# Folding the first two batches on TensorE, and new slots for the transforms of the others

## The chip, the cores and the metric

The kernel runs on one core of one Trainium2 chip. The metric is the device time of one execution in microseconds (us); lower is better. Before the change it was 667.26 us (median of three runs, 667.0 to 668.79). PE is TensorE, DVE is VectorE, ACT is ScalarE, POOL is GpSimd, SP is SyncE; PSUM is what TensorE writes to. The kernel's inputs and output stay in DRAM.

## The reference

Two stages, one after the other: the real part of a 2D Fourier transform of each of 8 batches, and a gated two-layer network on every token.

```python
def _attn_ref(x):                      # x: 8 x 3008 x 256, float32
    X = np.fft.fft(x, axis=1)
    X = np.fft.fft(X, axis=2)
    return X.real.astype(np.float32)

def _moe_ref(x, w_gate, w_val, w_out): # 24064 tokens, 256 -> 1536 -> 256
    g = x @ w_gate
    gelu = 0.5 * g * (1.0 + erf(g / sqrt(2)))
    val = x @ w_val
    return (gelu * val @ w_out).astype(np.float32)
```

## The kernel before

The transform is made of matmuls. Its input is first *folded*: each row of x is added to its mirror in time and in channel, which halves the work that follows. So x is loaded twice, forward by a plain DMA from SP's queue and mirrored by a gather from POOL's queue. Each load of 8 of the 17 parts is 768 KB. Batch 0 is folded on DVE, all others on POOL.

```python
    raw = [const_pool.tile([NPX, NJ, C], FP32, name=f"x_raw{i}") for i in range(2)]  # forward, mirror
    def load_part(b, k):
        j0, nj = ((9, 8), (1, 8), (0, 1))[k]
        load_forward(b, j0, nj)        # SP queue, 768 KB
        load_mirror(b, j0, nj)         # POOL queue, gather
    def fold_ops(b, j0, nj, eng):
        # ... first, second: sums over time and channel of raw[FORWARD], raw[MIRROR]
        if half_folded(b):             # b < 2: the last combination is left to the channel stage
            return [first, second]
        return [first, second, combine(0, ALU.add), combine(1, ALU.subtract)]
```

Then come stage 1 (over time), the channel stage, and the last stage (`tp_e`, `tp_o`), whose results ACT copies from PSUM into `EO_sb`, the input of the network. Three groups of columns are made per batch. For one row of `O` the copy is not enough: `tp_y` computes it, writes it to DRAM (`yrow`), and `tp_rows` reads it back, spread over all partitions into `EB_sb` and into one row of `EO_sb`.

```python
    def s1(b, jg, g, engine="A"):                       # stage 1, batches 0 and 1
        # ...
            for q, js in enumerate(JG[jg]):
                for j in js:
                    nc.tensor.matmul(ps[:, q * 96 : (q + 1) * 96], eo[:, j, g, :], G[:, j, :], ...)
    def tp_y(b, gi):
        # ... a 4 x 128 matmul, copied to yr, then
            nc.sync.dma_start(out=<4 x 128 of yrow in DRAM>, in_=yr[:, :])
    def tp_rows(b, gi):
        # ...
            nc.sync.dma_start(out=<EB_sb, group gi, 128 partitions>, in_=<yrow>)
            nc.sync.dma_start(out=<EO_sb, O half, group gi, 1 partition>, in_=<yrow>)
```

The network is 288 blocks in a row, 36 for each batch. A block makes one gelu pair. I call a block a *slot* and count them from 0. The rest of the work is hung into slots by a plan. The transform of batch b runs in the 36 slots of the network of batch b-1, so batch 2's in slots 36 to 71.

```python
    def plan():                                         # fill[s], pool[s]: work of slot s
        # ...
        for b in range(1, B):
            s0 = (b - 1) * NS                           # NS = 36
            # ops: 20 folds (10 for b = 1)
            first, n = {1: (11, 5), 2: (24, 28)}.get(b, (s0 - 16, 32))
            slot_of = [first + i * n // len(ops) for i in range(len(ops))]
            # ...
            if b + 1 < B:
                for k, piece in ((0, 1), (1, 3), (2, 4)):
                    at(fill, slot_of[piece * per + 1] + 1, lambda b=b, k=k: load_part(b + 1, k))
            # ... stage 1 after the folds; then the 9 items tp_y, tp_e, tp_o of 3 groups,
            #     the last of them in slot s0 + 33, about one a slot; tp_rows one slot after each group
```

## Time and profile before

Each line of the page gives busy times or shares of the span. First the page of the kernel before: busy time of PE and of ACT, PE's busy share in 40 equal slices (a digit is tenths), the clock that PE was granted in the same slices, and the chain of work that ended last.

```profile
span 666.5 us, 12960 instructions
PE 622.6 (93%) x4253; PEld 411.0 (62%) x4253; DVE 585.4 (88%) x946; ACT 432.0 (65%) x843; POOL 505.9 (76%) x509
PE   2888999999979999899979999799999999999997
...
PEclk9998999999989999899998999899999999999999
...
PE 76%; POOL 6%; DMA 6%; ACT 4%; issue 3%; DVE 2%; SPq 1%; POOLq 0%; ACTq 0%; DVEq 0%
```

PE is the engine that is full, but after its opening it falls to 7, 8, 7 and 7 in four slices some 80 us apart (a slice is 16.7 us; they begin at 183, 267, 333 and 417 us), and in each of them or the next one the clock falls to 8. In a single-core kernel that is PE-bound almost everywhere, the thing to read is where PE is *not* busy. The Trainium skill says in "Perfetto Trace Analysis", Identifying the Most-Contended Engine, that busy time of matmuls is a poor measure of distance to the roofline; that agrees here, since in the last of the windows at the end of this section PE is busy 2.00 of 2.00 us at half of its clock.

The chain of waits in order of time (start, length, what) names the gaps. These are its DMA pieces:

```profile
178.97 8.65 DMA EO_sb<-yrow
258.96 8.31 DMA EO_sb<-yrow
338.58 8.29 DMA EO_sb<-yrow
419.77 7.99 DMA EO_sb<-yrow
```

Around the first of them, the timeline shows who waited. Columns are start, busy time, engine, line and operation, what is written and read, and in brackets the engine's idle time before it with what ended it. SPq and POOLq lines are DMA issues; the data lands later.

```profile
177.30 0.95 POOL L145 DMA_INDIRECT x_raw<-in_x_dram,idx  x1
...
177.86 0.53 SPq L139 DMA_DIRECT2D x_raw<-in_x_dram  x1
178.49 0.40 SPq L555 DMA_DIRECT2D EB_sb<-yrow  x1
178.97 0.23 SPq L557 DMA_DIRECT2D EO_sb<-yrow  x1
179.42 0.25 SPq L547 DMA_DIRECT2D yrow<-yrow_sb  x1
...
187.71 0.57 ACT L521 ACTIVATE EO_sb<-ps_dft 128x481 bf16<-128x481 f32 x1 [4.60 <-DMA EO_sb<-yrow]
188.18 0.57 ACT L605 ACTIVATE gelu_sb<-ps_g 128x481 bf16<-128x481 f32 x1
...
189.26 0.77 PE L589 MATMUL ps_g<-EO_sb,W_sb 128*128 128x481 bf16 x3 [3.96 <-ACT gelu_sb L614]
```

The gather and the forward load of batch 4 start at 177.3 and 177.9; right behind them, after the row's read into `EB_sb`, goes the read of the one row of `EO_sb` (issued 178.97; I call it the row read), which lands at 187.6. ACT's copy of the next group into the same tile waits for it 4.6 us, both gelus stand behind the copy in ACT's order, and PE idles 4 us. What that does to the clock is in the busy time by windows. A line has the window, then busy time (and instructions) of PE, weight loads, DVE, ACT and POOL, then the granted clock, the DMA share and GB/s.

```profile
186.00:188.00 2.00, 0.00 (x0) 0.00 (x0) 0.19 (x1) 0.29 (x1) 0.55 (x1) 1.00 0.90 200
190.00:192.00 2.00, 2.00 (x12) 1.25 (x10) 1.20 (x2) 1.02 (x3) 0.39 (x1) 0.64 0.20 30
192.00:194.00 2.00, 2.00 (x7) 0.89 (x6) 1.11 (x3) 1.60 (x3) 1.12 (x2) 0.50 0.13 33
```

After 4 us without work, PE is granted half of its clock for some 3.4 us. That is the clock gate that the Trainium skill describes in "TensorE: Matmul & The Clock Gate", Part 1.

### The profile page before, as it was taken

What the parts mean: (1) busy time and instruction counts of PE and PEld (TensorE: products, weight loads), DVE (VectorE), ACT (ScalarE), POOL (GpSimd) and SP (SyncE); (2) the same over time, 40 slices, a digit from 0 to 9 for tenths busy, and PEclk for the clock granted to TensorE, in tenths of its full rate; (3) what the DMA queues carried; (4) which work ended last, traced back from release to release, by engine and by line L of the source; (5) the groups of instructions that cost most, each with busy time, mean ns of one, the idle gap of its engine ahead of it and who ended that gap; (6) DMA issues with size and microseconds to landing.
All of it is one profiled execution on the core that took longest, in us unless ns stands there. A gap on an engine that the chain in (4) does not pass through costs nothing.

```text
span 666.5 us, 12960 instructions
## 1 busy us (share of the span) xinstructions
PE 622.6 (93%) x4253; PEld 411.0 (62%) x4253; DVE 585.4 (88%) x946; ACT 432.0 (65%) x843; POOL 505.9 (76%) x509
## 2 busy tenths in 40 slices
PE   2888999999979999899979999799999999999997
PEld 1544666666646666566656666466666666666666
DVE  7697799999969998699968999699999999999992
ACT  3685676766746665666656667476677766766661
POOL 8449789988969699686987879688799865556551
PEclk9998999999989999899998999899999999999999
DMA  9942715453435336253361642626322133211112
GB/s 216 223 106 60 186 45 130 108 141 106 100 83 129 96 102 144 54 130 101 98 148 33 146 124 64 142 51 170 104 61 53 40 92 95 60 45 43 49 48 77
DMA packets 52332, 66.74 MB, mean 100 GB/s; under 512 B 7865, under 2 KB 47180, under 8 KB 49580
## 3 DMA queue, kind: packets, MB, share of 16 engines
q1 hardware_dynamic: 46024, 49.69, 28.7%
q0 software_dynamic: 5648, 15.73, 10.6%
q8 instruction: 33, 0.54, 0.4%
q10 hardware_dynamic: 592, 0.49, 0.3%
q14 instruction: 35, 0.29, 0.1%
HBM read 38.86 MB, written 29.38 MB: 102 GB/s over the span
## 4 chain that ended last, share of the span: by engine, by line
PE 76%; POOL 6%; DMA 6%; ACT 4%; issue 3%; DVE 2%; SPq 1%; POOLq 0%; ACTq 0%; DVEq 0%
PE ps_o L662 31%; PE ps_g L589 24%; PE ps_v L589 15%; DMA EO_sb<-yrow 5%; POOL h_sb L638 2%; PE ps_dft L475 2%; POOL eo_sb L194 2%; ACT gelu_sb L614 1%; ACT gelu_sb L605 1%; PE ps_dft L511 1%; SPq L583 1%; POOL x_raw L145 1%; PE ps_dft L456 1%; DMA out_dram<-out_sb 1%; DVE v_sb L636 1%
## 5 line engine op out<-in xcount | busy, mean ns | idle before, releaser
L638 POOL TENSOR_TENSOR h_sb<-gelu_sb,v_sb 128x512 bf16<-128x512 bf16 (+1 forms) x288 | 329.2, 1145 | 141.6 <-DVE v_sb L636 115.4
L662 PE MATMUL ps_o<-Wo_sb,h_sb 128*128 128x256 bf16 (+1 forms) x2232 | 338.8, 275 | 0.0
L662 PEld LDWEIGHTS <-h_sb 128*128 128x128 bf16 (+1 forms) x2304 | 231.0, 101 | 114.3 <-issue 4.0
L623 DVE SCALAR_TENSOR_TENSOR ve_sb<-EB_sb,yw,ps_v 128x512 f32<-128x512 bf16 (+1 forms) x288 | 212.3, 737 | 56.7 <-PE ps_v L589 55.5
L589 PE MATMUL ps_g<-EO_sb,W_sb 128*128 128x512 bf16 (+1 forms) x864 | 234.0, 380 | 16.4 <-ACT gelu_sb L614 16.3
L605 ACT ACTIVATE gelu_sb<-ps_g 128x512 bf16<-128x512 f32 (+1 forms) x288 | 169.7, 589 | 88.5 <-PE ps_g L589 85.5
L589 PE MATMUL ps_v<-EO_sb,W_sb 128*128 128x512 bf16 (+1 forms) x576 | 216.9, 380 | 0.5 <-ACT W_sb L390 0.5
L634 DVE TENSOR_TENSOR h_sb<-gelu_sb,ps_v 128x512 bf16<-128x512 bf16 (+1 forms) x288 | 195.3, 678 | 4.4 <-PE ps_v L589 3.4
L589 PEld LDWEIGHTS <-W_sb 128*128 128x128 bf16 x1440 | 137.4, 98 | 97.6 <-issue 20.2
L636 DVE SCALAR_TENSOR_TENSOR v_sb<-ve_sb,ps_v 128x512 f32<-128x512 f32 (+1 forms) x288 | 192.8, 670 | 0.0
L614 ACT ACTIVATE gelu_sb<-ps_g 128x512 bf16<-128x512 f32 (+1 forms) x288 | 169.2, 588 | 0.0
L681 ACT ACTIVATE out_sb<-ps_o 128x512 f32<-128x512 f32 x92 | 54.9, 597 | 40.6 <-PE ps_o L662 40.5
L194 POOL TENSOR_TENSOR eo_sb<-ab_sb 94x512 bf16<-94x512 f32 (+1 forms) x60 | 66.6, 1110 | 0.1
L521 ACT ACTIVATE EO_sb<-ps_dft 128x512 bf16<-128x512 f32 (+1 forms) x44 | 25.9, 589 | 31.0 <-DMA EO_sb<-yrow 17.4
L478 ACT ACTIVATE S_sb<-ps_dft 96x512 bf16<-96x512 f32 x48 | 28.4, 591 | 26.2 <-PE ps_dft L475 26.2
L187 POOL TENSOR_TENSOR ab_sb<-x_raw,x_raw 94x508 f32<-94x508 f32 (+1 forms) x30 | 32.9, 1097 | 0.0
L190 POOL TENSOR_TENSOR ab_sb<-x_raw,x_raw 94x508 f32<-94x508 f32 (+1 forms) x30 | 32.9, 1096 | 0.0
L145 POOL DMA_INDIRECT x_raw<-in_x_dram,idx x27 | 26.1, 966 | 5.4 <-issue 1.5
L475 PE MATMUL ps_dft<-eo_sb,G 94*96 94x256 bf16 x102 | 19.0, 272 | 2.0 <-POOL eo_sb L194 2.0
L511 PE MATMUL ps_dft<-TP,Z_sb 128*128 128x128 bf16 (+1 forms) x188 | 18.2, 220 | 1.0 <-DVE Z_sb L463 1.0
L511 PEld LDWEIGHTS <-Z_sb 128*128 128x128 bf16 x192 | 15.0, 100 | 3.0 <-DVE Z_sb L463 1.2
L475 PEld LDWEIGHTS <-G 94*96 94x96 bf16 x102 | 12.0, 124 | 3.2 <-issue 2.8
(117 smaller groups left out, 157.9 us busy)
## 6 DMA issues: line engine op xcount, KB each, us to landing
out_dram<-out_sb SPq DMA_DIRECT2D x361, 64.0 KB
x_raw<-in_x_dram SPq DMA_DIRECT2D x12, 768.0 KB
Z_sb<-z SPq DMA_DIRECT2D x6, 768.0 KB
z<-S_sb SPq DMA_DIRECT2D x6, 576.0 KB
EB_sb<-yrow SPq DMA_DIRECT2D x14, 128.0 KB
x_raw<-in_x_dram SPq DMA_DIRECT2D x2, 640.0 KB
x_raw<-in_x_dram SPq DMA_DIRECT2D x3, 384.0 KB
z<-S_sb SPq DMA_DIRECT2D x6, 192.0 KB
```

The lines of the kernel that those rows point to most:

```text
L194: eng.tensor_tensor(_sub(eo, [[C, nj], [1, 128]], j0 * C + g * 128), ab(0, 0, [[1, 128]]), ab(1, 0, [[1, 128]]), op=op)
L475: nc.tensor.matmul(ps[:96, q * C : (q + 1) * C], G[:, j, :], _sub(eo, [[1, C]], j * C), start=(j == js[0]), stop=(j == js[-1]))
L511: nc.tensor.matmul(ps[:, o : o + n], st["Z"][:, pair, g * 128 : g * 128 + 128], _sub(TP, [[1, n]], g * 128), start=True, stop=True)
L589: nc.tensor.matmul(ps[:, :n], W[nm, part][:, fs], src, start=start, stop=stop, **kw)
L605: nc.scalar.activation(gl[:, 0, :n], pg[:, :n], AF.Gelu)
L614: nc.scalar.activation(_sub(gl, [[-1, n]], TOK + n - 1), pg[:, :n], AF.Gelu)
L623: nc.vector.scalar_tensor_tensor(ve[:, :n], EB_bufs[b][:, c0 : c0 + n], yw[:, fc : fc + 1], pv[:, :n], op0=ALU.mult, op1=ALU.add)
L634: nc.vector.tensor_tensor(st["h"][:, fc, 0, :n], gl[:, 0, :n], pv[:, :n], op=ALU.mult)
L636: nc.vector.scalar_tensor_tensor(_sub(vv, [[-1, n]], n - 1), ve[:, :n], 2.0, pv[:, :n], op0=ALU.mult, op1=ALU.subtract)
L638: nc.gpsimd.tensor_tensor(st["h"][:, fc, 1, :n], gl[:, 1, :n], vv[:, :n], op=ALU.mult)
L662: nc.tensor.matmul(pso[:m, half], st["h"][:, fc, sign, h0 : h0 + m], Wo_sb[:, fc, :], start=(fc == 0), stop=(fc == NFC - 1),)
L681: nc.scalar.activation(_sub(osb, [[1, 2 * C]], 0, part_num=m), pso[:m, :], AF.Copy)
```

## The change

The intent, in the words of its author: "First two batches' x cast to bf16 by DMA and folded by TensorE (over t in stage 1, over c in the channel stage), no folds on DVE; transform begun 6 slots sooner". So the change has two parts. In the first, batches 0 and 1 are no longer folded by DVE and POOL: DMAs cast x to bf16 (three DVE copies cast a part of batch 0's), and stage 1 accumulates forward and mirrored x in PSUM with a second (negated) copy of G, 68 matmuls of 192 columns per batch instead of 34 of 96. With it come 12 matmuls on zeros at the start (*dummies*, whose result nobody reads) and other slots for the loads and the transform of batch 1 and the load of batch 2. In the second, folds and transforms of batches 2 to 7, and with them the loads of batches 3 to 7, get other slots. The diff, cut to its core:

```diff
-    def s1(b, jg, g, engine="A"):
+    def s1(b, jg, half, hl, engine="A"):
...
-            for q, js in enumerate(JG[jg]):
+            for q, js in enumerate(JG[jg][2 * half : 2 * half + 2]):
                 for j in js:
-                    nc.tensor.matmul(
-                        ps[:, q * 96 : (q + 1) * 96], eo[:, j, g, :], G[:, j, :],
-                        start=(j == js[0]), stop=(j == js[-1]))
+                    for i in range(2):
+                        src = _sub(xb[b], [[1, 128]], (i * NJ + (16 - j if i else j)) * C + hl * 128, part_num=NP)
+                        nc.tensor.matmul(
+                            _sub(ps, [[192, 2], [1, 96]], q * 96), src, _sub(G, [[96 * i, 2], [1, 96]], j * 192),
+                            start=(j == js[0] and i == 0), stop=(j == js[-1] and i == 1))
...
+    def cast_forward(b, j0, nj):
+        nc.gpsimd.dma_start(out=<xb[b], bf16>, in_=<x, float32>)
...                                   # opening()
+        idle = gelu_tile()[:, 0, :]
+        nc.vector.memset(idle, 0.0)
+        ps = psum("o")
+        for _ in range(12):
+            nc.tensor.matmul(ps[:, :], idle[:, 0:128], idle[:, :], start=True, stop=True)
...
-        for b in range(1, B):
+        units = [s1(1, jg, half, hl) for jg in (2, 1, 0, 3) for half in range(2) for hl in range(2)]
+        for i, f in enumerate(units):
+            at(fill, 8 + i // 2, f)
...
+        for b in range(2, B):
             s0 = (b - 1) * NS
...
-            first, n = {1: (11, 5), 2: (24, 28)}.get(b, (s0 - 16, 32))
+            first, n = (s0 - 16, 29) if b == 2 else (s0 - 22, 32)
...
+            spread(b, items, s + 7, s0 + NS - 3)      # one of the 9 items every second slot
```

The slot of the x load of the next batch hangs on `first`. For b of 3 and more it moves, like the folds, from s0 - 7 to s0 - 13.

More of the change, by code (lines that the diff above doesn't have):

```diff
@@ L74 @@
     dram_pool = ctx.enter_context(tc.tile_pool(name="dram", bufs=1, space=bass.MemoryType.DRAM))
-    G = const_pool.tile([NP, NJ, 4 * NK], BF16)
+    G = const_pool.tile([NP, NJ, 2, 4 * NK], BF16)
     TP = const_pool.tile([128, 2, 2, K1], BF16)
     CW = const_pool.tile([128, 2, 2, 128], BF16)
-    II = const_pool.tile([128, 2, 2, 128], BF16)
+    II = const_pool.tile([128, 3, 129], BF16)
     W_sb = const_pool.tile([128, 5, F], BF16)
@@ L86, in work, with xb_tile, raw_tile, stage_tile @@
         return work_pool.tile(shape, dt, tag=tag, bufs=bufs, name=name)
-    raw = [const_pool.tile([NPX, NJ, C], FP32, name=f"x_raw{i}") for i in range(2)]
+    def xb_tile(b):
+        return work([NPX, 2, NJ, C], BF16, f"raw{b}", 1, f"xb{b}")
+    raw = {}
+    def raw_tile(i):
+        if i not in raw:
+            raw[i] = work([NPX, NJ, C], FP32, f"raw{i}", 1, f"x_raw{i}")
+        return raw[i]
+    def stage_tile():
+        return work([NPX, 9, C], FP32, "h", 2, "x_stage")
     eo = const_pool.tile([NP, NJ, 2, 128], BF16, name="eo_sb")
@@ L94, in A_tile @@
     def A_tile():
-        return work([128, 2, NK, K1], BF16, "A", 1, "A_sb")
+        return work([128, 2, 2, NK // 2, 2 * K1], BF16, "A", 1, "A_sb")
     def S_tile():
@@ L139, in load_forward @@
             nc.sync.dma_start(
-                out=_sub(raw[FORWARD], [[1, nj * C]], j0 * C, part_start=p0, part_num=n),
+                out=_sub(raw_tile(FORWARD), [[1, nj * C]], j0 * C, part_start=p0, part_num=n),
                 in_=ap_replace(
@@ L152, in load_mirror @@
         gather(
-            _sub(raw[MIRROR], [[1, nj * C]], i0 * C),
+            _sub(raw_tile(MIRROR), [[1, nj * C]], i0 * C),
             ap_replace(x, ap=[[32 * C, B * NP], [1, 32 * C]]), idx[:NPX, :], (b * T + o) * C)
@@ L160, in load_part, with cast_mirror @@
         load_mirror(b, j0, nj)
-    def half_folded(b):
-        return b < 2
+    xb = {}
+    def cast_forward(b, j0, nj):
+        nc.gpsimd.dma_start(
+            out=_sub(xb[b], [[1, nj * C]], j0 * C),
+            in_=ap_replace(x, ap=[[32 * C, NPX], [1, nj * C]], offset=x.offset + (b * T + j0) * C))
+    def cast_mirror(b, j0, nj):
+        i0, o, idx = (16, 0, idx_0) if j0 == 0 else (17 - j0 - nj, 33 - j0 - nj, idx_x)
+        gather(
+            _sub(xb[b], [[1, nj * C]], (NJ + i0) * C),
+            ap_replace(x, ap=[[32 * C, B * NP], [1, 32 * C]]), idx[:NPX, :], (b * T + o) * C)
     def fold_ops(b, j0, nj, eng):
@@ L170, in fwd @@
         def fwd(c0, pat):
-            return _sub(raw[FORWARD], [[C, nj]] + pat, j0 * C + c0, part_num=NP)
+            return _sub(raw_tile(FORWARD), [[C, nj]] + pat, j0 * C + c0, part_num=NP)
         def mir(c0, pat):
-            return _sub(raw[MIRROR], [[-C, nj]] + pat, (16 - j0) * C + c0, part_num=NP)
+            return _sub(raw_tile(MIRROR), [[-C, nj]] + pat, (16 - j0) * C + c0, part_num=NP)
         def ab(q, c0, pat):
-            if half_folded(b):
-                return _sub(eo, [[C, nj]] + pat, j0 * C + q * 128 + c0)
             return _sub(st["ab"], [[C, nj]] + pat, q * 128 + c0)
@@ L183, in first @@
         def first():
-            if not half_folded(b):
-                st["ab"] = ab_tile()
+            st["ab"] = ab_tile()
             eng.tensor_tensor(ab(0, 0, [[128, 2]]), fwd(0, [[128, 2]]), mir(0, [[128, 2]]), op=ALU.add)
@@ L197, in combine @@
             return run
-        if half_folded(b):
-            return [first, second]
         return [first, second, combine(0, ALU.add), combine(1, ALU.subtract)]
@@ L207 @@
     row_k = const_pool.tile([128, NK], FP32)
-    row_c = const_pool.tile([128, 128], FP32)
+    row_c, row_r = (const_pool.tile([128, 128], FP32, name=f"row{i}") for i in range(2))
     par = const_pool.tile([1, 5, 128], FP32)
@@ L254, in pool_consts2 @@
             nc.gpsimd.memset(par[:, 0, r : r + 2], v)
+        nc.gpsimd.iota(row_r, pattern=[[-1, 128]], base=128, channel_multiplier=0, **IOTA)
+        nc.gpsimd.memset(row_r[:, 0:1], 0.0)
         nc.gpsimd.iota(row_t, pattern=[[1, K1]], base=0, channel_multiplier=0, **IOTA)
     def vec_fills():
-        nc.vector.memset(G[:, 0, 2 * NK :], 0.0)
-        nc.vector.memset(G[:, 16, 0 : 2 * NK], 0.0)
+        nc.vector.memset(G[:, 0, 0, 2 * NK :], 0.0)
+        nc.vector.memset(G[:, 16, 0, 0 : 2 * NK], 0.0)
         nc.vector.memset(one, 1.0)
@@ L297, in g_sin @@
             nc.scalar.activation(
-                _sub(G, [[96, nj], [2 * NK, 2], [1, NK]], j0 * 96 + h * NK),
+                _sub(G, [[192, nj], [2 * NK, 2], [1, NK]], j0 * 192 + h * NK),
                 _sub(rd, [[NK, nj], [NGP, 2], [1, NK]], j0 * NK, part_num=NP),
@@ L303, in g_sin_ends @@
         nc.scalar.activation(
-            _sub(G, [[NK, 2], [1, NK]], 16 * 96 + 2 * NK), _sub(rd, [[NGP, 2], [1, NK]], 16 * NK, part_num=NP),
+            _sub(G, [[NK, 2], [1, NK]], 16 * 192 + 2 * NK), _sub(rd, [[NGP, 2], [1, NK]], 16 * NK, part_num=NP),
             AF.Sin, scale=sc_g[:NP, 0:1])
@@ L309, in g_sin_ends, with g_negative @@
                 AF.Sin, scale=sc_g[:NP, h : h + 1])
+    def g_negative(j0, nj):
+        nc.vector.tensor_scalar(G[:, j0 : j0 + nj, 1, :], G[:, j0 : j0 + nj, 0, :], -1.0, None, op0=ALU.mult)
     def cw_phases():
@@ L330, in identities @@
     def identities():
-        for i in range(4):
-            nc.vector.tensor_scalar(
-                II[:, i // 2, i % 2, :], row_c, col_p, (1.0, 1.0, 1.0, -1.0)[i], op0=ALU.is_equal, op1=ALU.mult)
+        for i, (row, sign) in enumerate(((row_c, 1.0), (row_r, 1.0), (row_r, -1.0))):
+            nc.vector.tensor_scalar(II[:, i, 0:128], row, col_p, sign, op0=ALU.is_equal, op1=ALU.mult)
+            if i < 2:
+                nc.vector.memset(II[:, i, 128:129], 0.0)
+                nc.vector.memset(II[0:1, i, 128:129], 1.0 - 2 * i)
     def t_columns():
@@ L412, in ps_any @@
     def ps_any(b):
-        if b == 0 and turn[0] < 12:
+        if b == 0 and turn[0] < 20:
             turn[0] += 1
@@ L431, in run @@
             ps = ps_any(b)
-            for q, js in enumerate(JG[jg]):
+            for q, js in enumerate(JG[jg][2 * half : 2 * half + 2]):
                 for j in js:
-                    nc.tensor.matmul(
-                        ps[:, q * 96 : (q + 1) * 96], eo[:, j, g, :], G[:, j, :],
-                        start=(j == js[0]), stop=(j == js[-1]))
-            src = _sub(ps, [[1, 12], [12, 32]], 0)
-            dst = _sub(st["A"], [[128, 12], [1, 32]], g * NK * K1 + 32 * jg)
+                    for i in range(2):
[3 more added lines that the diff above has]
+                            start=(j == js[0] and i == 0), stop=(j == js[-1] and i == 1))
+            src = _sub(ps, [[192, 2], [1, 12], [12, 16]], 0)
+            dst = _sub(st["A"], [[NK * K1, 2], [128, 12], [1, 16]], 2 * hl * NK * K1 + 32 * jg + 16 * half)
             if engine == "A":
@@ L453, in run @@
             for q in range(2):
-                k = 2 * (2 * pp + q)
-                for g in range(2):
-                    nc.tensor.matmul(
-                        ps[:, q * C : (q + 1) * C], _sub(A, [[1, 128]], g * NK * K1 + k * K1), II[:, g, :, :],
-                        start=g == 0, stop=g == 1)
+                for o, n, d, ms in (
+                        (0, 129, 0, (II[:, 0, :], II[:, 1, :])),
+                        (129, 127, 1, (II[:, 0, 1:128], II[:, 2, 1:128]))):
+                    for hl in range(2):
+                        nc.tensor.matmul(
+                            ps[:, q * C + o : q * C + o + n], A[:, hl, d, 2 * pp + q, :], ms[hl],
+                            start=hl == 0, stop=hl == 1)
             dst = _sub(st["Z"], [[1, 512]], pp * 512)
@@ L475, in run @@
                     nc.tensor.matmul(
-                        ps[:96, q * C : (q + 1) * C], G[:, j, :], _sub(eo, [[1, C]], j * C),
+                        ps[:96, q * C : (q + 1) * C], G[:, j, 0, :], _sub(eo, [[1, C]], j * C),
                         start=(j == js[0]), stop=(j == js[-1]))
@@ L697, in opening @@
     def opening():
-        last2 = [(3, 2), (1, 2)]
-        for piece in (PIECES[0], PIECES[4], PIECES[1], PIECES[2], *last2):
-            load_forward(0, *piece)
+        stage = stage_tile()
+        xb[0] = xb_tile(0)
+        for j0, nj, at in ((9, 8, 0), (0, 1, 8)):
+            nc.sync.dma_start(
+                out=_sub(stage, [[1, nj * C]], at * C),
+                in_=ap_replace(x, ap=[[32 * C, NPX], [1, nj * C]], offset=x.offset + j0 * C))
+        pool_consts()
         index_consts(0)
-        load_mirror(0, *PIECES[0])
-        pool_consts()
+        cast_mirror(0, 9, 8)
         index_consts(1)
-        load_mirror(0, *PIECES[4])
-        load_mirror(0, *PIECES[1])
+        cast_mirror(0, 0, 1)
+        cast_forward(0, 1, 8)
         pool_consts2()
-        for piece in (PIECES[2], *last2):
-            load_mirror(0, *piece)
+        cast_mirror(0, 5, 4)
+        cast_mirror(0, 1, 4)
         for f0, n in ((0, 256), (256, 256), (512, 1024)):
@@ L713, in opening @@
             load_wo(q)
+        idle = gelu_tile()[:, 0, :]
[3 more added lines that the diff above has]
+            nc.tensor.matmul(ps[:, :], idle[:, 0:128], idle[:, :], start=True, stop=True)
+        vec_consts()
+        g_phases()
         vec_fills()
-        vec_consts()
         nc.vector.tensor_scalar(keep2, col_p, 1.0, None, op0=ALU.min)
         nc.vector.tensor_scalar(keep2, keep2, -2.0, None, op0=ALU.mult)
-        g_phases()
-        cw_phases()
         g_sin(9, 7)
@@ L722, in opening, with stage_cast, stage1 @@
         g_sin(1, 8)
-        cw_sin()
-        def fold_piece(j0, nj):
-            for f in fold_ops(0, j0, nj, nc.vector):
-                f()
+        def stage_cast(j0, nj, at):
+            nc.vector.tensor_copy(
+                _sub(xb[0], [[1, nj * C]], j0 * C), _sub(stage, [[1, nj * C]], at * C))
+        def stage1(jg, half):
+            s1(0, jg, half, 0)()
+            s1(0, jg, half, 1, "V")()
+        stage_cast(9, 4, 0)
+        stage_cast(13, 4, 4)
+        stage_cast(0, 1, 8)
+        g_negative(9, 8)
         t_columns()
         t_phases()
+        g_negative(0, 9)
+        cw_phases()
         t_sin()
+        cw_sin()
+        gelu_table()
+        stage1(2, 0)
+        stage1(2, 1)
         identities()
+        stage1(3, 0)
+        stage1(3, 1)
         cw_rest()
-        fold_piece(*PIECES[0])
-        gelu_table()
-        fold_piece(*PIECES[4])
-        for g in range(2):
-            s1(0, 3, g)()
-        fold_piece(*PIECES[1])
-        for g in range(2):
-            s1(0, 2, g)()
-        t_write()
-        fold_piece(*PIECES[2])
-        for g in range(2):
-            s1(0, 1, g)()
-        fold_piece(*last2[0])
-        fold_piece(*last2[1])
-        for g in range(2):
-            s1(0, 0, g, "AV"[g])()
+        t_write()
+        stage1(1, 0)
+        stage1(1, 1)
+        stage1(0, 1)
+        stage1(0, 0)
         ch(0, 0)()
@@ L757, in opening @@
         make_yw(0, 256)()
-        nc.sync.dma_start(out=sink, in_=Wo_sb[0:1, NFC - 1, C - 1 : C])
-        for k in range(3):
-            load_part(1, k)
     NS = NG * NFC
@@ L781, in plan, with second_x, spread @@
         for i, f in enumerate(early):
-            at(fill, (4, 5, 6, 8, 9, 10, 10, 11, 11, 12)[i], f)
-        for b in range(1, B):
+            at(fill, (3, 4, 5, 6, 6, 7, 8, 10, 11, 12)[i], f)
+        def second_x():
+            xb[1] = xb_tile(1)
+            cast_forward(1, 9, 8)
+        for s, f in (
+                (0, second_x), (1, lambda: cast_mirror(1, 9, 8)), (2, lambda: cast_forward(1, 0, 9)),
+                (3, lambda: cast_mirror(1, 5, 4)), (4, lambda: cast_mirror(1, 1, 4)),
+                (5, lambda: cast_mirror(1, 0, 1))):
+            at(fill, s, f)
+        units = [s1(1, jg, half, hl) for jg in (2, 1, 0, 3) for half in range(2) for hl in range(2)]
+        for i, f in enumerate(units):
+            at(fill, 8 + i // 2, f)
+        for k, s in ((0, 16), (1, 16), (2, 17)):
+            at(fill, s, lambda k=k: load_part(2, k))
+        def spread(b, items, s0, s1):
+            each = len(items) // NG
+            for i, f in enumerate(items):
+                s = s0 + i * (s1 - s0) // (len(items) - 1)
+                at(fill, s, f)
+                if i % each == each - 1:
+                    at(fill, s + 1, tp_rows(b, i // each))
+        items = []
+        for gi in range(NG):
+            items += [ch(1, 2 * gi), ch(1, 2 * gi + 1), tp_y(1, gi), tp_e(1, gi), tp_o(1, gi)]
+        spread(1, items, 16, NS - 3)
+        for b in range(2, B):
             s0 = (b - 1) * NS
@@ L795, in plan @@
                     at(fill, slot_of[piece * per + 1] + 1, lambda b=b, k=k: load_part(b + 1, k))
+            s = s0 - 9
+            for i, (jg, piece) in enumerate(((2, 1), (1, 2), (0, 3), (3, 4))):
+                ready = slot_of[piece * per + per - 1] + 1
+                for g in range(2):
+                    s = max(s + 1, ready)
+                    at(fill, s, s1t(b, jg, g))
+                if i == 2:
+                    at(fill, s + 1, z_write(b, 0, 12))
+                if i == 3:
+                    at(fill, s + 1, z_write(b, 12, 4))
+            at(fill, s + 3, z_read(b))
             items = []
-            for jg, piece in ((2, 1), (1, 2), (0, 3), (3, 4)):
-                ready = slot_of[piece * per + per - 1] + 1
-                items += [(ready, (s1 if b == 1 else s1t)(b, jg, g)) for g in range(2)]
-            each = 5 if b == 1 else 3
             for gi in range(NG):
-                fs = [tp_y(b, gi), tp_e(b, gi), tp_o(b, gi)]
-                if b == 1:
-                    fs = [ch(b, 2 * gi), ch(b, 2 * gi + 1)] + fs
-                items += [(0, f) for f in fs]
-            s = s0 + (11 if b == 1 else 0)
-            end = s0 + NS - 3
-            for i, (ready, f) in enumerate(items):
-                s = max(s + (0 if b == 1 and i in (1, 3, 5, 7) else 1), ready)
-                if i >= 8:
-                    s = max(s, end - (len(items) - 1 - i) * 8 // 7)
-                    if b > 1:
-                        s = max(s, at_read + 4)
-                at(fill, s, f)
-                if b > 1 and i == 5:
-                    at(fill, s + 1, z_write(b, 0, 12))
-                if b > 1 and i == 7:
-                    at(fill, s + 1, z_write(b, 12, 4))
-                    at_read = s + 3
-                    at(fill, at_read, z_read(b))
-                if i >= 8 and (i - 8) % each == each - 1:
-                    at(fill, s + 1, tp_rows(b, (i - 8) // each))
-            assert s <= end, (b, s, end)
+                items += [tp_y(b, gi), tp_e(b, gi), tp_o(b, gi)]
+            assert s + 7 < s0 + NS - 10
+            spread(b, items, s + 7, s0 + NS - 3)
         return fill, pool
```

## The prediction

> **What bounds the kernel now.** Span 666.5 us; PE is busy 93% (page, part 1). A slot is one FFN block (one gelu pair); first gelus in the timeline give its length: 1.96 us without a transform. PE loses time in four places:
>
> 1. *Batch boundaries.* The chain of waits has four 8.0 to 8.7 us pieces "DMA EO_sb<-yrow" (at 179, 259, 339, 420 us). In the timeline, a 768 KB load of x (issued 177.9) and its mirror gather go out just ahead of the small row read (issued 179.0), which lands at 187.6. ACT's copy to EO_sb waits for it 4.6 us, the gelus wait behind, PE stands idle 4.0 us and then gets a clock of 0.64 and 0.50 for 4 us (busy time by windows). The last 12 slots of such a batch take 30.0 to 30.9 us; without an x load nearby (batch 6) 24.9. Together 21 us, and 3 us in the following blocks. The drop agrees with the Trainium skill, "TensorE: Matmul & The Clock Gate", HAM clock gate (an idle array falls to half rate).
> 2. *Slots 12 to 35* take 58.7 us: PE waits for POOL's folds of batch 1, clock 0.83 in 60:70.
> 3. *Slots 0 to 11* (26.3 us) are ACT-bound (9.7 of 10 us busy in 30:40).
> 4. *Opening*: 27.4 us to the first FFN matmul, its second half a DVE chain (constants, folds, to 20.4 us).
>
> **What the change does.**
> - Opening: DVE folds (5.3 us) go; three casts, the negated G and seven more 0.56 us PSUM copies come: the same DVE total, but constants begin 1.5 us sooner. x is still 3.3 MB at about 245 GB/s, last landing now 17.05. Estimate -1.2 us.
> - Slots 0 to 11: batch 1's stage 1 becomes 16 evacuations of 0.49 us (8 before), half of them in slots 8 to 11, where ACT is tight. Estimate +1.7.
> - Slots 12 to 35: no POOL folds for batch 1. PE work (estimate): 24 slots 46.3, eight stage-1 units of four 192-column matmuls 2.7, channel and last transform 4.9: 54. 58.7 becomes 55, -3.7.
> - Batches 3 to 6: transform begun sooner and spread. The x load now goes out right after the first group's row read, five slots (10 us) ahead of the second's; the copy that waits comes five slots later still. Three of four stalls vanish: -16.9, and -1 in following blocks.
> - Batch 2: its first row read still goes out one slot after an x load; the waiting copy comes five slots after that load instead of four. The stall shrinks from 4.6 to 2.5 us, short enough to keep the clock: -3.5.
>
> Sum -24.6: **643 us**, range 634 to 656. Chances: faster by over 2% 0.84, within 2% 0.15, slower 0.01.
>
> **What would show each step.** Right: no long "DMA EO_sb<-yrow" in the chain for batches 3 to 6; ACT's wait for it down from 17.4 us to under 4; PE clock 0.9 or more throughout; first FFN matmul at 25.5 to 26.5; slots 0 to 11 at 27 to 29 us. Wrong: row reads still landing 8 us late; ACT waiting for PSUM or DMA in slots 8 to 25.
>
> **What would make it wrong.** Casting DMAs from one queue slower than 245 GB/s (x late, +2 to +5); the slot-16 burst holding up row reads or stores (+2 to +4); stalls moved to another x load, not removed (+5 each).

A remark on its words: the four stalls fall in the transforms of batches 2, 3, 4 and 5 (before the slots 72, 108, 144 and 180). What it calls "batches 3 to 6" are the three stalls at 108, 144 and 180.

## The result, and the profile after

The changed kernel takes 646.56 us (median of 4 runs, 645.99 to 646.81) against 667.68 us for the kernel before in the same rounds. The ratio is 0.9681, with a 95% interval of 0.9664 to 0.9698. Ratios are the mean time of one kernel's fast runs over the mean of the other's of the same rounds, so not quite the ratio of the medians.

The lines of the page that answer to those above, for the changed kernel:

```profile
span 644.7 us, 13198 instructions
PE 628.5 (97%) x4381; PEld 420.7 (65%) x4381; DVE 586.0 (91%) x944; ACT 434.4 (67%) x852; POOL 496.8 (77%) x498
PE   7988999999999999999999999999999999999997
...
PEclk8699999999999999999999999999999999999999
...
PE 86%; ACT 4%; POOL 3%; DVE 2%; DMA 2%; issue 1%; SPq 0%; ACTq 0%; POOLq 0%; DVEq 0%
```

The four dips between opening and end are gone, in PE's row and in the clock's, but the clock shows a dip at the start. (The kernel before has it too, as we shall see; its page doesn't show it.) PE is busy 6 us *longer* and yet the span is 22 us shorter. The waits (who waited for whom: total, times, longest, in us) had this line before:

```profile
ACT EO_sb L521 <- DMA EO_sb<-yrow: 17.4, 4, 4.6
```

After, no such line is left; the longest that ACT's copy waits is

```profile
ACT EO_sb L553 <- PE ps_dft L543: 21.2, 38, 0.6
ACT EO_sb L553 <- PE ps_o L694: 2.0, 1, 2.0
```

The first of the two is the ordinary wait for the matmul. The second is one wait of 2 us, which we shall meet again. The table gives the time between first gelus, worked out from the two traces, so that every microsecond of the span is in one row.

| stretch | before | after | difference |
|---|---|---|---|
| start to first gelu | 28.0 | 28.8 | +0.8 |
| slots 0 to 11 | 26.3 | 29.2 | +2.9 |
| slots 12 to 35 | 58.7 | 55.4 | -3.2 |
| slots 36 to 59 | 49.9 | 50.9 | +1.0 |
| slots 60 to 71 (stall, batch 2) | 30.0 | 26.2 | -3.8 |
| slots 96 to 107, 132 to 143, 168 to 179 (stalls, batches 3 to 5) | 91.6 | 74.8 | -16.7 |
| the 12 slots after each stall | 102.5 | 99.2 | -3.3 |
| the 12 slots after those | 96.0 | 97.6 | +1.5 |
| slots 204 to the end | 183.5 | 182.5 | -1.0 |

Differences are taken before rounding. The first three rows are the batches folded on TensorE: together +0.5 us. All of the gain stands in the rows about the stalls.

### The profile page after: what moved, and what is told of

It reads as the page before. It is cut to its first block, busy times and chain, and to the rows that moved or that the text cites. A ratio compares the mean times of both kernels' runs of the same rounds, so it can differ in the third digit from the quotient of the medians.

```text
span 644.7 us, 13198 instructions
## 1 busy us (share of the span) xinstructions
PE 628.5 (97%) x4381; PEld 420.7 (65%) x4381; DVE 586.0 (91%) x944; ACT 434.4 (67%) x852; POOL 496.8 (77%) x498
## 4 chain that ended last, share of the span: by engine, by line
PE 86%; ACT 4%; POOL 3%; DVE 2%; DMA 2%; issue 1%; SPq 0%; ACTq 0%; POOLq 0%; DVEq 0%
PE ps_o L694 35%; PE ps_g L621 27%; PE ps_v L621 17%; PE ps_dft L507 2%; DMA out_dram<-out_sb 2%; PE ps_dft L543 1%; ACT gelu_sb L637 1%; POOL eo_sb L214 1%; POOL h_sb L670 1%; PE ps_dft L463 1%; ACT gelu_sb L646 1%; PE ps_dft L488 1%; DVE v_sb L668 1%; PE ps_dft L410 1%; PE ps_dft L573 0%
## 5 line engine op out<-in xcount | busy, mean ns | idle before, releaser
L694 PE MATMUL ps_o<-Wo_sb,h_sb 128*128 128x256 bf16 (+1 forms) x2232 | 334.7, 273 | 0.0
L621 PE MATMUL ps_g<-EO_sb,W_sb 128*128 128x512 bf16 (+1 forms) x864 | 230.7, 376 | 0.8 <-ACT gelu_sb L646 0.5
L621 PE MATMUL ps_v<-EO_sb,W_sb 128*128 128x512 bf16 (+1 forms) x576 | 214.5, 375 | 0.0
L158 POOL DMA_INDIRECT x_raw<-in_x_dram,idx x18 | 17.1, 949 | 2.9 <-issue 1.1
L463 PEld LDWEIGHTS <-xb 94*128 94x128 bf16 x136 | 15.4, 121 | 4.7 <-issue 3.6
```

The source lines that it names most:

```text
L621: nc.tensor.matmul(ps[:, :n], W[nm, part][:, fs], src, start=start, stop=stop, **kw)
L694: nc.tensor.matmul(pso[:m, half], st["h"][:, fc, sign, h0 : h0 + m], Wo_sb[:, fc, :], start=(fc == 0), stop=(fc == NFC - 1),)
```

## The experiments

Each kernel gave correct results and ran on the chip beside the kernel before, whose median was 667.23 to 667.52 us.

**1. Only the x load moved.** Theory: the stall is the x load in front of the row read. Rivals: the transform is too late as such, or the gain comes from TensorE.

```diff
 # kernel before
-  at(fill, slot_of[piece * per + 1] + 1, lambda b=b, k=k: load_part(b + 1, k))
+  at(fill, slot_of[piece * per + 1] + 1 + (8 if b > 2 and k == 0 else 0), lambda b=b, k=k: load_part(b + 1, k))
```

> The kernel before, with one edit: the first x load for batches 4 to 7 goes out 8 slots later, one slot after the batch boundary and behind all row reads of that boundary. Theory 1 (the row read is stuck behind the x load, and nothing else is wrong at the boundary): all four stalls go, the last 12 slots of those batches take 24.9 us instead of 30.0 to 30.9, the total falls by 20 to 25 us to 643 to 648, with no other part of the change in it. Theory 2 (the transform as such is begun too late, the row read would be late anyway): stalls of 4 us stay, total 662 to 668. Theory 3 (the gain of the change comes from folding on TensorE): total stays at 667.

Measured: 647.06 us (645.61 to 647.08), ratio 0.9679 (0.9653 to 0.9706). The four boundary stretches take 24.88 us each, and no wait of ACT for the row is left. These are this kernel's waits of the copies and of yrow:

```profile
ACT EO_sb L521 <- PE ps_dft L511: 15.0, 30, 0.9
ACT yrow_sb L545 <- PE ps_dft L541: 10.5, 20, 0.5
```

So moving four loads (each a forward load and a gather) by eight slots, in an otherwise unchanged kernel, gives as much as the whole change. Theories 2 and 3 fall as explanations of the gain.

**2. Only the new slots.** The kernel before with the loop over batches 2 to 7 of the changed kernel (its `first`, `n` and `spread`); batches 0 and 1 are folded as before.

> The kernel before, with only the new slots for batches 2 to 7 (folds from 22 slots ahead of the batch, items spread); batches 0 and 1 are folded on DVE and POOL as before. Theory 1: the whole gain is here, total 644 to 649. Theory 3: total stays at 662 to 668.

Measured: 646.93 us (646.5 to 647.64), ratio 0.9675 (0.9648 to 0.9702). The whole gain is here.

**3. Only TensorE folding.** The changed kernel with the old loop over batches 2 to 7.

> The changed kernel, with the slots of folds, loads and transforms of batches 2 to 7 put back as they were before; casting DMAs and TensorE folding of batches 0 and 1 stay. Theory 1 (the gain comes from the slots): the four stalls return, total 664 to 670. Theory 3 (the gain comes from TensorE folding and the casts): total stays near 647. The difference to the kernel before is what TensorE folding of batches 0 and 1 is worth by itself; from the two traces (opening +0.8, slots 0 to 11 +2.9, slots 12 to 35 -3.2) I expect +0.5 us, that is within 2 us of 667.7.

Measured: 672.18 us (668.82 to 672.98), ratio 1.0059 (1.0029 to 1.0089). The four stalls are back:

```profile
ACT EO_sb L553 <- DMA EO_sb<-yrow: 17.9, 4, 4.8
```

The expectation of 664 to 670 was missed by 2 us, and so was that of at most 2 us from the kernel before. The trace is of the fastest of the four runs (668.82 us), and its span is 0.2 us longer than that of the kernel before; the three slower runs (671.5 to 672.98, with a mean clock of 0.967 to 0.969 against 0.973) have no trace, so where their 3 to 4 us went is open. What stands is that the casts and TensorE folding, as they are in the change, gain nothing by themselves: measured alone, they are 0.6% slower.

**4. The row read in another queue.** Is the row late because it stands behind the load in SP's queue, or because the DMA engines are full?

```diff
 # kernel before, tp_rows
-            nc.sync.dma_start(
+            nc.scalar.dma_start(
                 out=_sub(EO_bufs[b], [[1, n]], HALF + chunk_off[gi], part_num=1),
```

> The kernel before, with one edit: the small row read into EO_sb is issued from ACT's queue instead of SP's; times of all loads are kept. If the row read is late because it stands behind the 768 KB load in the same queue, it now lands in 2 to 3 us, the four stalls go and the total is 644 to 650. If it is late because all 16 DMA engines are full with the x load, whichever queue it is in, it still lands 6 to 9 us late and the total stays at 660 to 668. Issuing costs ACT some 0.3 us 21 times, which should not show.

Measured: 657.65 us (656.6 to 659.67), ratio 0.9848 (0.9813 to 0.9882): between the two. The timeline of this kernel at the first boundary shows why (ACTq is an issue in ACT's queue):

```profile
177.03 0.20 ACTq L557 DMA_DIRECT2D EO_sb<-yrow  x1
177.11 0.53 SPq L139 DMA_DIRECT2D x_raw<-in_x_dram  x1
182.70 0.57 ACT L521 ACTIVATE EO_sb<-ps_dft 128x481 bf16<-128x481 f32 x1 [0.33 <-PE ps_dft L511]
...
187.35 0.21 ACTq L557 DMA_DIRECT2D EO_sb<-yrow  x1
187.66 0.57 ACT L605 ACTIVATE gelu_sb<-ps_g 128x481 bf16<-128x481 f32 x1 [3.47 <-DMA yrow<-yrow_sb]
```

The copy that used to wait 4.6 us now waits for its matmul alone. But the third group's row is still *written* to DRAM through SP's queue, behind the load (issued 178.67, landed 187.27, by the chain of waits). ACT's queue, which must now issue the read of that row, waits for the write, and the gelu waits behind it. The stall was moved from one small transfer behind the load to the next. And the edit did more than change the queue: the read now goes out some 0.08 us *before* the forward load (at all four boundaries), where it went out 1.1 us behind it, and its packet ran at 178.08 us, before the first packet of the gather (178.4) and of the load (179.2). So this experiment shows that a row read in front of the load is in time, and not what another queue does for one behind it.

**5. Both the write and the read of the row in ACT's queue.**

```diff
 # kernel of experiment 4, tp_y
-            nc.sync.dma_start(
+            nc.scalar.dma_start(
                 out=ap_replace(y, ap=[[128, 4], [1, 128]], offset=y.offset + chunk_off[gi]), in_=yr[:, :])
```

> The kernel before, with both ends of the row's way on ACT's queue: the write of the row to DRAM (yrow) and the read into EO_sb. With the read alone on ACT's queue, ACT's copy no longer waited, but the next group's write of the row stayed behind the x load in SP's queue (issued 178.7, landed 187.3) and ACT's queue waited for it (9.8 us in three waits, total 657.7). If queue order is the whole cause, now no wait for yrow of over 1 us is left and the total is 644 to 648. If full DMA engines are also part of it, some 3 us stay at each boundary and the total is 652 to 660.

Measured: 651.97 us (651.67 to 652.6), ratio 0.9766 (0.9751 to 0.9781). Better again, but 5 us short of experiment 1. At the first boundary:

```profile
177.78 0.53 SPq L139 DMA_DIRECT2D x_raw<-in_x_dram  x1
...
179.35 0.25 ACTq L547 DMA_DIRECT2D yrow<-yrow_sb  x1
...
187.06 0.22 ACTq L557 DMA_DIRECT2D EO_sb<-yrow  x1
187.38 0.57 ACT L605 ACTIVATE gelu_sb<-ps_g 128x481 bf16<-128x481 f32 x1 [2.51 <-PE ps_o L662]
```

The write is now alone in its queue, issued 1.6 us behind the load, and ACT's next issue still comes 7.7 us later. (The profile puts the gelu's wait down to a matmul that was done long before.) The trace's packet records bear it out: the four 256-byte packets of this write began between 184.3 and 185.5 us, while the packets of the gather and of the forward load ran from about 179 to 186. In experiment 4, where the same write stood behind the load in SP's queue, its packets began 7.2 us after the issue, here 5.0 us. So a queue of its own brings a small transfer behind the load forward by some 2 us, and its waiter by some 1 us (7.7 us against 8.6). Of the 5.7 us gained over experiment 4, some 3.4 are the clock: that trace has two stretches of 3.4 us at half clock behind the boundaries, this one none (an estimate: each costs half of its length).

So the 10 us of experiment 4 can't be put down to the queue, since the read had also got in front, and what the queue is worth to a transfer behind the load is the smaller part. That the load's packets keep the DMA engines busy meanwhile (their mean busy share is 0.95 to 1.09 from 179 to 185 us) is the likely reason for the rest; no run tests it apart. The remedy that takes all of it is distance in time. The Trainium skill, "DMA: Bandwidth & Descriptors", Queues, rings and completion order, says that each DMA engine takes turns between queues by packets of many descriptors; these runs agree in that the write's packets ran while those of the load were still running, and show that taking turns doesn't keep a small transfer from being late.

**6. The stall that was left.** In the changed kernel, slot 64 takes 4.05 us. Its timeline has

```profile
166.44 0.53 SPq L152 DMA_DIRECT2D x_raw<-in_x_dram  x1
167.08 0.38 SPq L587 DMA_DIRECT2D EB_sb<-yrow  x1
167.55 0.24 SPq L589 DMA_DIRECT2D EO_sb<-yrow  x1
...
175.33 0.60 ACT L553 ACTIVATE EO_sb<-ps_dft 128x512 bf16<-128x512 f32 x1 [2.05 <-PE ps_o L694]
```

The same pattern, but the profile names a matmul as releaser. To test it, the load of batch 4 was moved two slots, behind the row read.

```diff
 # changed kernel
+  ... + (2 if b == 3 and k == 0 else 0)
```

> The changed kernel, with the first x load of batch 4 moved two slots later (slot 59 to 61), behind batch 2's first row read. In the changed kernel slot 64 takes 4.05 us and ACT's copy there begins 2.05 us late; the profile puts that wait down to a matmul. If it is the remaining case of a row read behind an x load, slot 64 falls to about 1.9 us and the total by about 2 us (646.6 to 644.5). If the wait is for the matmul that the profile names, nothing changes.

Measured: slot 64 takes 2.62 us instead of 4.05, slots 60 to 71 25.03 instead of 26.18, and in the trace the copy comes at 173.69 after an ordinary 0.61 us wait for its matmul. The total, 646.22 us (645.35 to 646.72), ratio 0.9675 (0.9656 to 0.9695), can't be told from the changed kernel's; the 1.2 us of the trace is within the spread of the runs (experiment 10 shows it better). The wait was the row read. In experiment 9's trace the same wait of 2.0 us, at the same place, is put down to the row read:

```profile
ACT EO_sb L553 <- DMA EO_sb<-yrow: 2.0, 1, 2.0
```

**7. The opening: is it worth warming PE up?** The clock in the changed kernel, by windows:

```profile
8.00:10.00 2.00, 1.50 (x14) 1.49 (x15) 1.77 (x5) 0.00 (x0) 1.92 (x7) 0.98 0.79 154
10.00:12.00 2.00, 2.00 (x15) 1.89 (x13) 1.78 (x8) 0.31 (x1) 1.71 (x3) 0.50 0.67 84
18.00:20.00 2.00, 2.00 (x15) 1.84 (x13) 1.06 (x3) 0.85 (x2) 1.32 (x2) 0.50 0.96 160
22.00:24.00 2.00, 1.82 (x17) 1.76 (x18) 0.12 (x1) 0.60 (x1) 0.00 (x0) 0.50 1.24 203
28.00:30.00 2.00, 1.95 (x15) 1.38 (x16) 0.75 (x1) 1.31 (x5) 0.00 (x0) 1.00 0.58 111
```

In its timeline, stage 1 of batch 0 is a row of such lines, one unit of four matmuls every 0.64 us, 160 ns for 192 columns:

```profile
18.12 0.84 PE L463 MATMUL ps_dft<-G,xb 94*128 94x192 bf16 x4
18.76 0.84 PE L463 MATMUL ps_g<-G,xb 94*128 94x192 bf16 x4
```

So 68 matmuls take 10.9 us (68 x 0.16), which, with a pause of 0.8 us, fills PE from 9.7 to 21 us. 192 columns in 160 ns is half clock, as in the Trainium skill, "TensorE: Matmul & The Clock Gate", Wait — 56ns, not 53.3ns? (start to start is columns over 1.2 GHz while cold, which is 160 ns for 192). The opening is bound by PE at half clock. The 12 dummies bring the clock to 1.0 only from 6.5 to 9.9 us (the trace's clock records), when PE waits for constants. First, without any dummies (one look):

> The changed kernel without the 12 dummy matmuls at the start. In its trace the granted clock is 1.0 only from 6.5 to 9.9 us, when PE mostly waits, and 0.5 for the whole of stage 1 (192-column matmuls 160 ns apart). If the dummies buy nothing, the first FFN matmul stays at 28.2 us within 0.3; if they do help the start of stage 1 or the constants, it comes at 29 or later.

Measured: 647.73 us in one run, whose state is unknown; the first gelu comes at 29.9 us against 28.8, the first matmul of the network at 29.45. So the second case of the expectation came true: the matmuls that make constants (L364) run 2.29 us without dummies and 1.27 with them, and that is the 1.0 us. Then 21 dummies, to close the pause before the constants:

> The changed kernel with 21 dummy matmuls in place of 12, so that PE has no 2 us pause between the dummies and the wait for the constants. Theory: the opening got slower (28.2 us to the first FFN matmul, against 27.4) because stage 1 runs at half clock after that pause. If the pause caused the drop and stage 1 itself can hold the clock, matmuls of stage 1 come 85 ns apart, stage 1 is then bound by its PSUM copies and by x arriving (last at 14.7 us), and the first FFN matmul comes at 22 to 25 us: total 641 to 644. If stage 1 can't hold the clock by itself, it drops again after one period of 3.4 us (at 13.3) and the total is 644 to 646.

Measured: 645.7 us (645.46 to 647.08), ratio 0.9674 (0.9651 to 0.9698). The first gelu comes at 27.9 us. Stage 1 starts at full clock, but the clock falls at 10.96 us all the same, 1.3 us into stage 1, and stays at half until 24.6. The total can't be told from the changed kernel's; the 0.9 us is the traces'. Before that fall PE still idled 1.1 us and ran one-column matmuls (the constants) for 1.2 us, so whether stage 1 by itself would hold the clock is open. But it doesn't raise it: from 14.3 to 21.3 us it runs without a pause, at half clock.

**8. Dummies within stage 1.** As 7, with one 512-column dummy after each of the 16 units.

```diff
 # changed kernel, with range(21)
         def stage1(jg, half):
             s1(0, jg, half, 0)()
+            nc.tensor.matmul(ps[:, :], idle[:, 0:128], idle[:, :], start=True, stop=True)
             s1(0, jg, half, 1, "V")()
+            nc.tensor.matmul(ps[:, :], idle[:, 0:128], idle[:, :], start=True, stop=True)
```

> As the one with 21 dummies, with one more 512-column dummy after each of the 16 units of stage 1. If stage 1 can't hold the clock by itself but a denser stream can, the clock stays at 1.0 through stage 1 and the first FFN matmul comes at 23 to 26 us, total 641 to 645. If the clock drops all the same, the 16 dummies cost 0.43 us each and the first FFN matmul comes at 30 us or later, total 648 to 655.

Measured: 643.52 us (643.08 to 643.74), ratio 0.9636 (0.9614 to 0.9657). The first gelu comes at 25.7 us, 3.1 us sooner than in the changed kernel, *with 25 more matmuls in front of it*. The windows of this kernel:

```profile
10.00:12.00 2.00, 2.00 (x19) 1.60 (x19) 1.75 (x9) 0.31 (x1) 1.71 (x3) 1.00 0.60 83
18.00:20.00 2.00, 1.94 (x19) 1.53 (x18) 1.12 (x2) 0.78 (x3) 1.21 (x2) 1.00 1.02 153
22.00:24.00 2.00, 1.80 (x22) 1.22 (x20) 1.68 (x3) 0.88 (x3) 0.00 (x0) 1.00 1.21 198
```

PE was about as busy in both kernels (2.00 of 2.00 in 18:20 in the changed kernel, 1.94 here), at half and at full clock. Stage 1 itself ends only 1.2 us sooner, since its second half still waits until 14.3 us; the rest of the 3.1 us is gained behind it, where the last matmuls of the opening now run at full clock too. What it is about stage 1 that keeps the clock down is open: its matmuls use 94 of 128 rows, and each loads new weights; the runs don't tell these apart.

**9. Slots 0 to 11.** I had predicted +1.7 us there from ACT's time. The trace has no full engine in slots 8 to 11:

```profile
48.00:58.00 10.00, 8.34 (x72) 5.48 (x70) 8.73 (x14) 7.92 (x18) 5.29 (x5) 1.00 0.00 1
```

All units of stage 1 go through two PSUM banks there, while the bank of the second layer (`o`) is idle until slot 12.

```diff
 # changed kernel
+        units = [s1(1, jg, half, hl, tag="o" if hl and jg in (2, 1) else None) ...]
```

> The changed kernel, with every other unit of batch 1's stage 1 in slots 8 to 11 put into the PSUM bank of the second layer, which is idle until slot 12; else all units share two banks. In the changed kernel slots 8 to 11 take 10.5 us (8.7 before), and no engine is over 90% busy there. If the two banks (matmuls wait for a copy, the copy for the matmuls) set the time, slots 8 to 11 fall to 8.8 to 9.5 us and the total by 1 to 1.7 us. If ACT's time sets it, as I predicted, they stay at 10.5 and the total at 646.6.

Measured: 644.52 us (643.72 to 645.37), ratio 0.9655 (0.964 to 0.9671). Slots 0 to 11 take 27.0 us instead of 29.2, slots 8 to 11 8.3 instead of 10.5. So in slots 8 to 11 it was the two banks, matmuls waiting for copies and copies for matmuls, and not ACT's time.

**10 and 11. All together.** `best` is 8 with 6; `best_o` has 9 too.

> The changed kernel with 21 dummies and one more after each unit of stage 1 (643.5 by itself, first FFN matmul 25.1 instead of 28.2) and with the x load of batch 4 two slots later (slots 60 to 71 25.0 instead of 26.2). The two lie in different stages, so they should add: 641.5 to 643.

> As best, with the third bank for batch 1's stage 1 as well. If the third bank helps, 640 to 641.5; if not, as best.

Measured: best 642.18 us (642.16 to 642.33), ratio 0.9617 (0.9603 to 0.963); best_o 640.09 us (640.07 to 640.22), ratio 0.9585 (0.9572 to 0.9598). Best is 1.3 us under experiment 8, which is experiment 6's trace difference. The gains add, as those of different stages should, and best_o beats the changed kernel by 6.5 us (1%). These runs also differ among themselves by 0.2 us only, where the others differ by 0.7 to 4.

## Why the prediction was right or wrong, point by point

- **The total** (643, range 634 to 656): measured 646.56. Right in the range; 3.6 us of the predicted gain of 24.6 is missing.
- **Boundary stalls**: right, and shown. Three of four vanish, as the load now goes out some 10 us before the next row read: predicted -16.9, measured -16.7. The following blocks: about -1 predicted for these three, -2.1 measured. Batch 2: -3.5 predicted (down from 4.6 to 2.5 us of waiting), measured 2.05 us of waiting and -3.8, with the following slots -5.0. Experiments 1 and 2 show that this alone is the gain, and experiment 1 that it is the load, not the 6 slots, that matters: the transform was not begun sooner there. The prediction says only that the load goes out just ahead of the row read, and that holds. What delays the read, its place in the queue or the busy DMA engines, is settled in part: experiment 5 gives the queue some 1 to 2 of some 8 us.
- **Opening**, predicted -1.2, measured +0.8: wrong in sign. The step of the prediction that failed is "DVE folds (5.3 us) go; [...] the same DVE total, but constants begin 1.5 us sooner". It took DVE and the DMAs as the limits and costed twice the matmuls of twice the columns at nothing. They were the new limit: PE worked on stage 1 from 9.7 to 21 us at half clock. The clock could have been read from the trace of before, where stage 1's 96-column matmuls come some 80 ns apart in the opening against 43 in the chain of waits near 70 us. The page shows a clock of 1.0 there, since the first clock record is made at 26.7 us.
- **Slots 0 to 11**, predicted +1.7, measured +2.9: the direction right, the reason wrong. In slots 8 to 11, where the prediction put its cost, it is +1.8, but "ACT is tight" should have been "two PSUM banks are tight": a third bank gives back 2.2 us. The other +1.2 stands in slots 0 to 7; it wasn't foreseen, and nothing was tried on it.
- **Slots 12 to 35**, predicted -3.7, measured -3.2: right. The waits for POOL's folds went and the longer stage 1 came; that the two are what made the difference was not tested apart.
- **Not foreseen**: +1.0 us in slots 36 to 59 and +0.4 us in each later batch's middle stretch, where spread items now stand. They come with the new slots (experiment 2 has them, with batches 0 and 1 unchanged), and nothing more was tried on them.
- **The worries** were not borne out: x of batch 0 was all there at 14.65 us (17.05 before), and the burst of loads at slots 16 and 17 made no copy late.

So the part of the change that its title puts first gains nothing as it stands, and an experiment with one moved line gains as much as all of it. With the dummies and the third bank, best_o is 6.8 us (646.93 to 640.09) better than experiment 2, of which some 1.2 is the moved load of batch 4. But it is not shown that this makes TensorE folding pay: 2.1 us of it are the opening (first gelu at 25.9 against 28.0 us), and a kernel that folds on DVE, with dummies in its own half-clock opening, was not tried.

## What to carry to other kernels

When a big load and a tiny transfer that someone waits for are issued side by side, put the tiny one first, or put some 10 us between them; another queue, for a transfer that stands behind the load, gave only 1 to 2 of some 8 us here. When PE seems busy in a profile's opening, divide a matmul's columns by its distance to the next before believing that the clock is full; dummy matmuls among thin ones may pay for themselves (25 of them brought the first gelu 3.1 us forward here). And try each part of a change alone: here the smallest part was the whole gain.

## What the Trainium skill lacked or had wrong

- "TensorE: Matmul & The Clock Gate", Part 1, says that the clock rises after some 3.4 us of sustained work. Here PE was busy 1.5 to 2.0 of every 2 us from 10 to 26 us and stayed at half clock for 17 us (9.9 to 27.0). Stage 1's matmuls (94 rows, 192 columns, new weights for each) did not raise it; with one 128-row, 512-column matmul after every four to six of them it stayed at 1.0 all through. Apart from transposes, the page doesn't say what counts as busy.
- "DMA: Bandwidth & Descriptors", Queues, rings and completion order, says that engines take turns between queues. It gives no number for a small transfer beside a large one: a 1 KB write alone in its queue, issued 1.6 us after a 768 KB load in another, had its packets run 5.0 us later, and its waiter was released after 7.7 us; behind the load in the same queue the packets ran 7.2 us later, and it took 8.6 us.
- "Perfetto Trace Analysis" doesn't warn that a wait's releaser, which a reader of traces infers, can be named wrongly: the 2.0 us wait of experiment 6 was put down to a matmul in one trace and to the row's DMA in another.
- No page says that a clock before a trace's first clock record is unknown: the page of the kernel before shows 1.0 up to its first record at 26.7 us, with 96-column matmuls some 80 ns apart against 43 later.
